# A gated state-space and MLP mix with its gradients on one core: the inverse scratch in 128-partition loads, the first chunk's tables beside the last inverse step, and a new order of loads and buffers in the tail

## The chip, the cores and the metric

The kernel runs on one core of a Trainium2 chip, in one launch. The metric is device time in microseconds, as the median over runs. A profiled execution gives the trace, whose span runs from the first to the last instruction.

## The reference

With `x = A_u` (2048 rows of 448), the reference computes a gate, a state-space long convolution and a squared-ReLU MLP, and the gradients of their mix:

```python
g = sigmoid((x * gate_w).sum(-1, keepdims=True))
# a: K[d, l] = Re sum_n C[d,n] exp(dt A[d,n] l) dt B[d,n],  N = 256, l < 2048
y = irfft(rfft(x, 4096) * rfft(K, 4096))[:2048]        # per channel d, causal convolution
a = bf16(y) + x * Dskip
# b: h = x' @ w1 + b1 (448 -> 1792);  b = relu(h)**2 @ w2 + b2 (1792 -> 448)
out = g * a + (1 - g) * b
```

Returned are `out` and 14 gradients for a given `grad_out`: those of `A_u`, of the real and imaginary parts of A, B and C (448 x 256 each), of `log_dt`, `Dskip`, `w1`, `b1`, `w2`, `b2` and `gate_w`.

## The kernel before

The convolutions go by a Fourier transform in two steps of 64 points as matmuls. `fwd1` multiplies the rows and stores its result to a DRAM scratch `gd`, which `load_s1` reads back in another order; `fwd2` (L253) makes the spectrum. A product with another spectrum follows, then `inv1` (L289), which stores to a scratch `hd`; `load_hs` (L300) reads `hd` back in four parts, and `inv2` (L307, L309) makes the rows of the output from them. The MLP's forward and backward pass is cut into "dense steps" (`N_(n)` does n units of them, `D_` as many as bring it to a quota): L651 and L654 are matmuls, L666 and L679 the evacuations on ScalarE, L687 a second group of matmuls.

Three stages follow one another.

*The front* (to about 215 us) loads inputs and tables and transforms the input and the weighted gradient. A scheduler sets the order of its instructions. The inverse transform of the kernel gradient, `inv1(q)` for q = 0 to 3, has dense steps between its parts. Then `tc.manual_schedule()` starts, and from there each engine does its instructions in the order in which the code names them.

*The middle* makes, in 14 chunks of states, the convolution kernel and the sums over positions for the parameter gradients. For each chunk, `load_x` (L1012) and `load_y` (L1017) read a record of powers, `neg_x` (L1020) and `seeds_x` (L1023) start the table X on ScalarE, `step_x` doubles it on VectorE (L991, L992, L994); `fields_y` (L1028 to L1035) copies fields on ScalarE, `seeds_y` (L1043) and five `build_y` (L1001, L1002, L1004) make the table Y. `kgen` (L1066) multiplies the tables into the convolution kernel, `k_out` (L1077) stores it to `k_d`, and `load_yt` (L1085, "LY") transposes Y with four DMA transposes on SP's queue. `step_sums` (L1166) is the `inv2` of the inverse transform in a form that picks the rows wanted: it reads all four parts of `hd`, evacuates (L1173) and passes the result through `dk_d` to the buffer DK. The opening of the middle does chunk 0 and half of chunk 1 by hand; then `period(c, tokens)` runs a list of tokens: Y0 to Y4, X0 to X2, KM, KO, LY, the sums Z0 to Z3, P0, P1, and D for dense steps.

*The tail* (from about 665 us) reads the finished kernel from `k_d` (`reload_k`, L1310 and L1316), transforms it (`fwd1`, L206 and L207 evacuate, L232 multiplies, L237 stores), runs the last chunk's LY and sums, and then for each q: `product` (L1478, L1479), `fwd2` of the next part, `back1` (an `inv1`). `back1(0, q)` stores the output's half, `back1(1, q)` the gradient's. Its staging buffers are four blocks `oq`. Output loop 0 (L1538, L1539, L1546 to L1551) makes out_0 and the gate's sums from `hs1`, with `ao = oq[q]` as its output buffer; output loop 1 (L1564) makes the gradient of `A_u` from `hs2`, with the parameter gradients (`param_grads`, L1395 to L1429) between as `Pg(n)`, which need `load_raw` (L1373) and `load_st` (L1379) for four blocks of channels. `load_rows16` (L351) fetches the gradient `Gt` and the input `U` again.

Of the kernel before, what the change touches and what calls it, by code (L numbers as in the profile page):

```python
# [19 lines left out]
P = 128  # L20
# [22 lines left out]
def host_consts():  # L43
# [42 lines left out]
    Et = np.zeros((2, 32, 2, 4, 8, 32), np.float64)  # L86
    k1 = np.arange(32)[:, None]
    l1 = np.arange(32)[None, :]
    for hp in range(2):
        for l0g in range(4):  # L90
            for x in range(8):
                l = 64 * l1 + 16 * l0g + 8 * hp + x
                C = (2.0 / 4096) * np.exp(2j * np.pi * (k1 + 0.5) * l / 4096)
                Et[hp, :, 0, l0g, x] = C.real
                Et[hp, :, 1, l0g, x] = -C.imag
    c["Etw"] = Et.reshape(128, 4 * 8 * 32)
# [29 lines left out]
def sum_consts():  # L126

    mats, places = {}, position_places()
    k1 = np.arange(32)
    for l, v in enumerate(rounded_positions()):  # L130
        l0 = l % 64
        C = (2.0 / 4096) * np.exp(2j * np.pi * (k1 + 0.5) * l / 4096)
        p, b = places[int(v)]
        e, i = (p // 2 % 2, 2 * (p // 4) + p % 2) if p < 16 else (p // 8, p % 8)
        row = 8 * sum_row(b) + i
        M = mats.setdefault((l0 % 8, l0 // 16, e, row // 32), np.zeros((2, 32, 2, 32)))
        M[l0 // 8 % 2, :, 0, row % 32] += C.real
        M[l0 // 8 % 2, :, 1, row % 32] -= C.imag
    keys = sorted(mats)
    return np.concatenate([mats[k].reshape(128, 32) for k in keys], axis=1), keys  # L140
# [22 lines left out]
class Ker:  # L163
# [133 lines left out]
    def load_hs(self, hd, q, hs):  # L297
        for hp in range(2):
            src = bass.AP(tensor=hd, offset=(32 * hp + 8 * q) * D, ap=[[64 * D, 64], [1, 8 * D]])
            self.nc.sync.dma_start(hs[64 * hp:64 * hp + 64].rearrange("p g x d -> p (g x d)"), src)  # L300

    def inv2(self, hs, q, x, hp, ps, more=()):

        nc = self.nc
        Et = self.Et[:].rearrange("p (g x m) -> p g x m", g=4, x=8)
# [9 lines left out]
def kernel(ctx, tc, A_u, A_A_re, A_A_im, A_B_re, A_B_im, A_C_re, A_C_im, A_log_dt, A_Dskip,  # L315
# [30 lines left out]
    def load_rows16(queues, dst, ap2d, halves=(0, 1)):  # L346

        for g in range(NG):
            for h in halves:
                src = bass.AP(tensor=ap2d.tensor, offset=ap2d.offset + (16 * g + 8 * h) * D, ap=[[64 * D, 32], [1, 8 * D]])  # L350
                queues[g % len(queues)].dma_start(flat(dst[32 * g:32 * g + 32, 8 * h:8 * h + 8]), src)  # L351
# [10 lines left out]
    cs["F1K"] = cs["F1BD"].reshape(4, 32, 256).transpose(1, 0, 2).reshape(128, 256)  # L362
# [12 lines left out]
    for h in range(2):  # L375
        for g in range(NG):
            src = bass.AP(tensor=u2.tensor, offset=u2.offset + (16 * g + 8 * h) * D, ap=[[64 * D, 32], [1, 8 * D]])
            (nc.sync if g % 2 == 0 else nc.scalar).dma_start(flat(U[32 * g:32 * g + 32, 8 * h:8 * h + 8]), src)
    ldb = const.tile([P, D], bf16, name="ldb")
# [86 lines left out]
    Fs = K.t("F17", [P, 8704])  # L466
# [80 lines left out]
    Fp = K.t("F17", [P, 8704])  # L547
# [412 lines left out]
    KW = K.t("K28", [P, 2 * NA * D])  # L960
    DK = KW[:, NA * D:].rearrange("p (a d) -> p a d", d=D)
    Y = K.t("Y16", [P, W2, 2, 64])
    XB = K.t("X16", [P, 8192])
    RB = K.t("R32", [P, 8, 2048])
    XW = [XB[:, 0:4096], RB[:, 4:6].rearrange("p k x -> p (k x)")]
    yring = [RB[:, k].rearrange("p (w n) -> p w n", n=P) for k in range(4)]
    KS = XB[:, 4096:4096 + NY * 80].rearrange("p (s c i q) -> p s c i q", s=NY, q=GC, i=CW)
    zrow = XB[0:48, 7680:8128]
    G_.memset(zrow, 0.0)
    nc.sync.dma_start(bass.AP(tensor=k_d, offset=16 * 48 * D, ap=[[D, 48], [1, D]]), zrow)  # L970
    G_.memset(Y[:].rearrange("p w t b -> p (w t b)").bitcast(fp32), 0.0)
    G_.memset(Y[:, :, 0, 0], 1.0)
    Fv = K.t("F17", [P, 8704])
# [21 lines left out]

    yb, vb = Y[:, 0, 0, 0:1], Vt[:, 0:1]

# [9 lines left out]
    Y4 = Y[:]  # L1007
# [3 lines left out]
    def load_x(c):  # L1011
        nc.sync.dma_start(rx_[:, 0:896], bass.AP(tensor=rec_d, offset=c * P * RS, ap=[[RS, P], [1, 896]]))  # L1012

    def load_y(c):
        nonlocal rec
        rec = K.t("rec", [P, 1024])
        nc.sync.dma_start(rec[:], bass.AP(tensor=rec_d, offset=c * P * RS + 896, ap=[[RS, P], [1, 1024]]))  # L1017
# [132 lines left out]
    def load_rows():  # L1150
        load_const("Ew", nc.sync)
        for b in (KW[:, 0:3584], KW[:, 3584:7168], R2[:, 0:3584], R2[:, 4096:7680]):
# [32 lines left out]

    R2 = RB.rearrange("p k x -> p (k x)")
    load_x(0)
    load_y(0)
    load_rows()
    for h in range(2):  # L1190
        G_.memset(KW[64 * h + 32:64 * h + 64, NA * D:].bitcast(fp32), 0.0)
    for i in range(3):
        fields_y(i)
# [24 lines left out]
    for v in range(3):  # L1218
        step_x(1, 2 << v, v)
        N_(1)  # L1220
    load_x(2)
    while acc[1]:
        N_(1)
    BK.update(h=("N0", "N1"), t="N2", a="N3")
    Pt = K.t("P14", [P, 7168])
# [62 lines left out]
    def period(c, tokens, k=0):  # L1288
        for o in tokens:
# [3 lines left out]
            elif c or o not in ("YS", "Y0", "Y1", "Y2", "Y3", "Y4", "LY"):  # L1293
                token(o, c)
    for lb in range(4):
        nc.sync.dma_start(dbt[lb], bass.AP(tensor=DBT_d, offset=lb * P * 2048, ap=[[2048, P], [512, DT], [1, 512]]))
    period(0, "KM KO D D D".split())
    period(1, "SP YS Y0 D Y1 Y2 WP Z0 D NX Y3 Y4 Z1 D KM KO Z2 L0 D Z3 L2 R P0 D SA P1 D X0 FY0 D S X1 D FY1 FY2 D X2 D WD".split())
    Fx, R2 = Fv, RB.rearrange("p k x -> p (k x)")
# [18 lines left out]
    def reload_k():  # L1318
        reload(64, 64, 0, 2, 32, (2, 4), (48, 16))
        reload(32, 32, 0, 4, 8, (4, 2), (48, 16))  # L1320
        reload(64, 64, 3, 1, 48 + 32, (2, 4), (48, 16))
        reload(32, 32, 7, 1, 48 + 8, (4, 2), (48, 16))
        fix(79, 16, 4, 3, 34, 2)
        fix(47, 16, 2, 7, 12, 20)
# [27 lines left out]
    period(NCH - 1, "LY P0 SA P1 S WD".split())  # L1352
# [12 lines left out]
    sx[0, 2] = load_sx(0, 2, 4)  # L1365
    Gt = Yf[:, 0:7168].rearrange("p (t d) -> p t d", d=D)
# [84 lines left out]
    M2v = Yf[:, 0:4096]  # L1451
    K.M2 = M2v

    def between(n):
        if n == 5:
            nc.sync.dma_start(M2v, cdr["M2"].ap())
    K.fwd1(lambda j: xv[:, JO.index(j)], gd[2], stage=stg + [K.t("st", [P, 4, D], bufs=2) for _ in range(2)], between=between)
    period(NCH, "Z0 Z1 Z2 P0 Z3 P1".split())
    sums = back_s(NCH - 1, [Qs.pop((NCH - 1, h)) for h in range(2)])
    s1k = [b.rearrange("p (a d) -> p a d", d=D) for b in (KW[:, 7168:10752], KW[:, 10752:14336], SB[:, 6272:9856], SB[:, 0:3584])]  # L1460
    for q in range(4):
        K.load_s1(gd[2], q, s1k[q])
# [8 lines left out]
    oq = [Fx[:, 1792 * i:1792 * i + 1792].rearrange("p (a d) -> p a d", d=D) for i in range(4)]  # L1471
# [16 lines left out]
    for q in range(4):  # L1488
# [8 lines left out]
        if q == 2:  # L1497
            load_st(0, SB[:, 9856:11904], G_)
            Pg(1)
            load_rows16((nc.sync,), Gt, G2, (0,))  # L1500
    hs1.append(load_hs(1, 0, 6))
    load_rows16((nc.sync,), Gt, G2, (1,))
    for q in range(4):
# [23 lines left out]
    for q in range(4):  # L1527
        hs = hs1[q]
        ao = oq[q]
        for x in range(2):  # L1530
            pp = K.pair()
            for hp in range(2):
# [4 lines left out]
                jk = XB[:, 7168 + 448 * (t % 2):7616 + 448 * (t % 2)]  # L1537
                V.scalar_tensor_tensor(out=jk, in0=ps, scalar=1.0, in1=Gt[:, t, :], op0=ALU.mult, op1=ALU.mult, accum_out=dg[:, t:t + 1])  # L1538
                V.scalar_tensor_tensor(out=ao[:, 2 * hp + x], in0=ps, scalar=g32[:, t:t + 1], in1=b0, op0=ALU.mult, op1=ALU.add)  # L1539
# [75 lines left out]
```

## Time and profile before

| | us |
|---|---|
| median of 3 runs (857.14 to 860.26) | 859.49 |
| profiled execution | 860.13 |
| its span | 858.4 |
| busy: PE, DVE, ACT, POOL | 642.5, 565.5, 514.1, 155.8 |
| DMA traffic | 181.59 MB, mean 212 GB/s |

PE is TensorE's matmuls, PEld its weight loads, DVE is VectorE, ACT ScalarE, POOL GpSimd, and SPq the queue of SyncE, which only issues DMAs here. Names such as L1166 are lines of the kernel before. In a line of waits, "A x <- B y: 13.7, 1, 13.7" says that A's instruction waited for B's: total us, times, the longest. In a timeline the columns are start, duration, engine, line, operation, output<-input and the number of instructions. PEclk is the granted TensorE clock as a share of full speed (0.852 in the mean); a DMA share of 1 means that all 16 DMA engines are busy.

### The profile page before, as it was taken

What the parts mean: (1) busy time and instruction counts of PE and PEld (TensorE: products, weight loads), DVE (VectorE), ACT (ScalarE), POOL (GpSimd) and SP (SyncE); (2) the same over time, 40 slices, a digit from 0 to 9 for tenths busy, and PEclk for the clock granted to TensorE, in tenths of its full rate; (3) what the DMA queues carried; (4) which work ended last, traced back from release to release, by engine and by line L of the source; (5) the groups of instructions that cost most, each with busy time, mean ns of one, the idle gap of its engine ahead of it and who ended that gap; (6) DMA issues with size and microseconds to landing.
All of it is one profiled execution on the core that took longest, in us unless ns stands there. A gap on an engine that the chain in (4) does not pass through costs nothing.

```text
span 858.4 us, 20221 instructions
## 1 busy us (share of the span) xinstructions
PE 642.5 (75%) x8433; PEld 337.7 (39%) x8477; DVE 565.5 (66%) x932; ACT 514.1 (60%) x869; POOL 155.8 (18%) x262
## 2 busy tenths in 40 slices
PE   3577957879467987997999976987999732973483
PEld 1122323323234554564655653544656411531011
DVE  4596686775733287958998985575779233692674
ACT  1596876686345774885788766774555123882153
POOL 3222101112414010111101020100001230115242
PEclk9977965988869998998999995997999965997556
DMA  9957667558979399999889989796997597979992
GB/s 185 244 146 251 230 227 285 199 203 290 241 144 240 69 261 198 251 207 201 195 202 214 182 194 215 142 189 138 189 217 204 133 218 251 390 210 288 257 305 59
DMA packets 209547, 181.59 MB, mean 212 GB/s; under 512 B 132160, under 2 KB 185993, under 8 KB 209199
## 3 DMA queue, kind: packets, MB, share of 16 engines
q1 hardware_dynamic: 187838, 124.93, 62.4%
q0 software_dynamic: 13408, 35.22, 14.2%
q10 hardware_dynamic: 8208, 20.14, 6.7%
q8 instruction: 66, 1.08, 0.5%
q14 instruction: 27, 0.21, 0.1%
HBM read 85.19 MB, written 64.32 MB: 174 GB/s over the span
## 4 chain that ended last, share of the span: by engine, by line
PE 35%; DMA 22%; DVE 14%; ACT 14%; issue 9%; SPq 3%; POOL 1%; ACTq 0%; POOLq 0%; DVEq 0%
PE psN L880 7%; PE psN L651 5%; PE psS L1138 4%; DMA R<-Y 3%; DMA hd<-F 3%; PE psX L1066 3%; PE psN L687 2%; DMA U<-rT_d 2%; SPq L1085 2%; DMA gd<-X 2%; DVE Y L1001 2%; PE psF L1110 1%; PE psX L687 1%; DVE F L1002 1%; DMA F<-rec_d 1%
## 5 line engine op out<-in xcount | busy, mean ns | idle before, releaser
L1112 ACT CAST P<-psF 128x1024 bf16<-128x1024 f32 x56 | 57.2, 1021 | 11.2 <-PE psF L1110 11.0
L687 PEld LDWEIGHTS <-U 128*128 128x128 bf16 x448 | 41.5, 101 | 40.5 <-issue 10.8
L651 PE MATMUL psN<-S 128*128 128x512 bf16 x151 | 47.3, 418 | 10.6 <-ACT st L1173 3.3
L1001 DVE TENSOR_TENSOR Y<-Y,F 128x1024 bf16<-128x1024 bf16 (+3 forms) x70 | 48.0, 686 | 3.1
L651 PEld LDWEIGHTS <-S 128*128 128x128 bf16 x336 | 30.4, 102 | 49.5 <-issue 25.2
L1004 DVE TENSOR_TENSOR Y<-Y,F 128x1024 bf16<-128x1024 bf16 (+3 forms) x70 | 48.1, 687 | 2.4
L687 PE MATMUL psN<-S,U 128*128 128x449 bf16 x224 | 47.9, 355 | 0.0
L1002 DVE TENSOR_TENSOR F<-Y,F 128x1024 bf16<-128x1024 bf16 (+3 forms) x70 | 47.3, 676 | 0.0
L1110 PE MATMUL psF<-S,R 41*128 41x32 bf16 x1792 | 32.0, 175 | 18.4 <-DVE S L1096 10.6
L1145 POOL DMA_DIRECT2D s_d<-st x28 | 14.0, 506 | 167.4 <-ACT st L1143 161.3
L880 PEld LDWEIGHTS <-U 128*128 128x128 bf16 x308 | 29.1, 102 | 32.1 <-issue 8.0
L880 PE MATMUL psN<-D,U 128*128 128x448 bf16 x168 | 39.8, 388 | 2.4 <-ACT U L865 2.1
L1110 PEld LDWEIGHTS <-R 41*128 41x128 bf16 x1792 | 27.7, 94 | 30.3 <-issue 26.4
L679 ACT ACTIVATE U<-psN 128x1024 bf16<-128x1024 bf16 x37 | 38.1, 1031 | 1.3 <-PE psN L678 1.3
L1043 DVE COPY Y<-rec 128x256 bf16<-128x256 bf16 x14 | 10.3, 737 | 42.3 <-PE psX L1066 24.1
L666 ACT ACTIVATE U<-psN,b_f 128x512 bf16<-128x512 f32 x44 | 28.6, 685 | 14.7 <-DVE st L535 7.5
L687 PE MATMUL psX<-D,U 128*128 128x448 bf16 x144 | 36.0, 391 | 0.7 <-ACT D L693 0.7
L1121 DVE TENSOR_TENSOR M<-P,X 128x2048 bf16<-128x2048 bf16 x14 | 17.1, 1221 | 26.9 <-ACT P L1112 26.9
L232 PEld LDWEIGHTS <-cb_F1BD 128*128 128x128 bf16 x96 | 10.3, 117 | 55.2 <-issue 45.4
L651 PE MATMUL psN<-K,S 128*128 128x512 bf16 x99 | 27.9, 394 | 4.8 <-issue 3.5
L865 ACT ACTIVATE U<-U 128x1792 bf16<-128x1792 bf16 x12 | 20.1, 1694 | 15.7 <-DMA U<-rT_d 15.7
L880 PE MATMUL psN<-S,U 128*128 128x448 bf16 x140 | 28.4, 353 | 0.0
(356 smaller groups left out, 1690.1 us busy)
## 6 DMA issues: line engine op xcount, KB each, us to landing
sp<-K ACTq DMA_DIRECT2D x8, 896.0 KB, 5.8
R<-hd SPq DMA_DIRECT2D x12, 448.0 KB, 13.7
U<-rT_d SPq DMA_DIRECT2D x6, 896.0 KB, 6.6
rT_d<-U POOLq DMA_DIRECT2D x10, 512.0 KB, 4.8
hd<-F SPq DMA_DIRECT2D x11, 448.0 KB, 12.8
U<-rT_d SPq DMA_DIRECT2D x9, 512.0 KB, 6.4
X<-gd SPq DMA_DIRECT2D x5, 896.0 KB, 4.8
U<-dhT_d SPq DMA_DIRECT2D x5, 896.0 KB, 5.7
```

Of the source, the lines that this page charges most:

```text
L651: T_.matmul(pss[k][:], lhsT=w[:, dt], rhs=x(2 * half + k)[:, dt], start=(dt == 0), stop=False, skip_group_check=True)
L666: S.activation(r[:, 512 * lb:512 * lb + 512], pss[k][:], ACT.Relu, bias=b1_f[:, j:j + 1])
L679: S.activation(hn[j % 2][:, 8 * th:8 * th + 8, :], ps[:], f)
L687: T_.matmul(ps[:, 0:w], lhsT=hn[j % 2][:, t, :], rhs=rhs[:, t, :], start=(t == 0), stop=(t == LT - 1))
L880: T_.matmul(ps[:, 0:D], lhsT=src[:, j, P * x:P * x + P], rhs=ws[:, j, :], start=(w == 1 and j == 0), stop=(j == FT - 1))
L1001: V.tensor_tensor(out=run(yb, dst, [64, X2], [d0[1], n // d0[1]], [1, d0[1]]), in0=run(yb, 0, [64, X2], *src), in1=pr, op=ALU.mult)
L1002: V.tensor_tensor(out=run(vb, 0, [n, X2], [d0[1], n // d0[1]], [1, d0[1]]), in0=run(yb, 0, [64, X2], *src), in1=pi, op=ALU.mult)
L1004: return V.tensor_tensor(out=hi, in0=hi, in1=run(vb, n, [2 * n, W2], [-n, 2], [1, n]), op=ALU.add)
L1066: T_.matmul(ps[32 * g:32 * g + 32, i], lhsT=run(xb, 2048 * (1 - t) + w, [W2, 32]), rhs=Y[:, w, t, 0:NY], start=(h == 0 and t == 0), stop=( ...
L1110: T_.matmul(psz[:, t, 32 * b:32 * b + 32], lhsT=yt[64 * t:64 * t + NY, b, :], rhs=DKc[64 * t:64 * t + NY, c % 2, 16 * (j % 2) + b].rearran ...
L1112: S.copy(run(zbs[c, h][:, 0:1], 16 * (j % 2), [1024, 2], [64, NA], [32, 2], [1, 16]), run(psz[:, 0, 0:1], 0, [512, 2], [1, NA], [NA, 2], [ ...
L1138: T_.matmul(sps[64 * h:64 * h + 64, cc, r, :], lhsT=Q[h][r][:, 1024 * t + 64 * a:1024 * t + 64 * a + 64], rhs=(nident if r == 0 and t == 1 ...
```

## The change

1. `load_hs` reads a part of `hd` in one DMA over 128 partitions, where there were two over 64. The table `Et` is padded with zeros to 128 rows for each half (2048 columns for 1024), and `inv2`'s matmuls read 128 rows instead of 64. `step_sums` gets its table in the same row order.
2. The input's rows are divided between the two queues as halves instead of alternately, and two buffers change their size or home.
3. The last inverse step is moved behind the start of the manual order; `load_x(0)`, `load_y(0)`, `neg_x` and two of the three table steps of chunk 0 are placed in it. The scratch parts 2 and 3 go to another buffer. The clearing of Y is split between VectorE and POOL. `load_x(1)` and `load_y(1)` go to POOL's queue. All five `build_y` with a dense step each, and the rest of the dense steps of the opening, come before `neg_x`, `seeds_x(1)` and `step_sums`; `kgen(0)` and `k_out` follow the sums directly. `period(0)` has only dense steps.
4. In the tail, the reloads have their two outer dimensions exchanged, with the table of the first transform permuted accordingly. The LY of the last chunk moves from before the transform to after it. The table M2 and one part of `gd` are loaded on POOL's queue. `Gt` and `oq` exchange buffers. Three parts of `hs1` are read before the second half of Gt, and three of `hs2` before output loop 0. `load_raw` and `load_st` of blocks 1 to 3 move from the `back1(1, q)` loop into output loop 0. The rows of Gt and U are divided between SP and POOL. In output loop 0, each VectorE operation of L1539 becomes a ScalarE copy with a scale, and one VectorE addition follows for each pair of tiles.

```diff
     def load_hs(self, hd, q, hs):
-        for hp in range(2):
-            src = bass.AP(tensor=hd, offset=(32 * hp + 8 * q) * D, ap=[[64 * D, 64], [1, 8 * D]])
-            self.nc.sync.dma_start(hs[64 * hp:64 * hp + 64].rearrange("p g x d -> p (g x d)"), src)
+        src = bass.AP(tensor=hd, offset=8 * q * D, ap=[[32 * D, P], [1, 8 * D]])
+        self.nc.sync.dma_start(hs.rearrange("p g x d -> p (g x d)"), src)
...
-            nc.tensor.matmul(ps[32 * l0g:32 * l0g + 32], lhsT=Et[64 * hp:64 * hp + 64, l0g, 2 * q + x, :],
-                             rhs=hs[64 * hp:64 * hp + 64, l0g, x, :],
-                             start=not more, stop=True, tile_position=(64 * hp, 32 * l0g), skip_group_check=bool(more))
+            nc.tensor.matmul(ps[32 * l0g:32 * l0g + 32], lhsT=Et[:, hp, l0g, 2 * q + x, :], rhs=hs[:, l0g, x, :],
+                             start=not more, stop=True, tile_position=(0, 32 * l0g), skip_group_check=bool(more))
...
-    for q in range(4):
-        if q < 3:
-            spectra(q + 1)
+    for q in range(3):
+        spectra(q + 1)
...
+    load_x(0)
+    load_y(0)
     neg_x()
-    for v in range(3):
-        tables_x(0, v)
+    def early(q2):
+        N_(IV[q2])
+        if q2 == 0:
+            tables_x(0, 0)
+            tables_x(0, 1)
+    K.inv1(Pc, 3, hd[0], between=early)
...
+    load_rows()
+    V.memset(Y[:, :, 0, 0], 1.0)
+    V.memset(Y[:, :, 1, 0], 0.0)
+    G_.memset(Y[:, :, :, NY:64], 0.0)
+    for i in range(3):
+        fields_y(i)
...
+    tables_x(0, 2)
+    load_x(1, G_)
+    N_(1)
+    seeds_y()
+    load_y(1, G_)
+    for v in range(5):
+        build_y(v)
         N_(1)
-    load_x(1)
-    seeds_y()
-    load_y(1)
+    while acc[1]:
+        N_(1)
     neg_x()
     seeds_x(1)
-    for v in range(2):
-        build_y(v)
-        N_(1)
     step_sums()
-    for v in range(2, 5):
-        build_y(v)
-        N_(1)
+    kps0 = kgen(0)
+    k_out(0, kps0)
     YTs[0] = [load_yt(j) for j in range(4)]
...
-    period(0, "KM KO D D D".split())
+    period(0, ["D"] * nd)
...
-        reload(64, 64, 0, 2, 32, (2, 4), (48, 16))
-        reload(32, 32, 0, 4, 8, (4, 2), (48, 16))
+        reload(64, 64, 0, 2, 32, (48, 16), (2, 4))
+        reload(32, 32, 0, 4, 8, (48, 16), (4, 2))
...
-    period(NCH - 1, "LY P0 SA P1 S WD".split())
+    period(NCH - 1, "P0 SA P1 S WD".split())
...
-    Gt = Yf[:, 0:7168].rearrange("p (t d) -> p t d", d=D)
+    Gt = Fx[:, 0:7168].rearrange("p (t d) -> p t d", d=D)
...
+    period(NCH - 1, ["LY"])
+    G_.dma_start(M2v, cdr["M2"].ap())
...
+    for q in range(4):
+        K.load_s1(gd[2], q, s1k[q], G_ if q == 0 else None)
     period(NCH, "Z0 Z1 Z2 P0 Z3 P1".split())
...
-    oq = [Fx[:, 1792 * i:1792 * i + 1792].rearrange("p (a d) -> p a d", d=D) for i in range(4)]
+    oq = [Yf[:, 1792 * i:1792 * i + 1792].rearrange("p (a d) -> p a d", d=D) for i in range(4)]
...
         back1(1, q)
-        if q < 3:
-            hs1.append(load_hs(1, q + 1, (4, 0, 1)[q]))
-        if q == 2:
-            load_raw(2, SB[:, 6272:7808], G_)
-            load_st(2, SB[:, 7808:9856], G_)
-    load_raw(1, SB[:, 3584:5120], G_)
-    load_st(1, SB[:, 9856:11904], G_)
-    load_raw(3, SB[:, 0:1536], G_)
-    load_st(3, SB[:, 1536:3584], G_)
+        if q == 0:
+            hs1.append(load_hs(1, 3, 1))
+    for q in range(3):
+        hs2.append(load_hs(2, q, (2, 5, 3)[q]))
...
-                V.scalar_tensor_tensor(out=ao[:, 2 * hp + x], in0=ps, scalar=g32[:, t:t + 1], in1=b0, op0=ALU.mult, op1=ALU.add)
-        hs2.append(load_hs(2, q, (2, 5, 3, 6)[q]))
-        if q == 3:
-            load_rows16((nc.sync,), Uv, u2)
+                S.activation(ao[:, 2 * hp + x], ps, ACT.Copy, scale=g32[:, t:t + 1])
+            V.tensor_tensor(out=ao[:, x:x + 3:2], in0=ao[:, x:x + 3:2], in1=br[0][:, 2 * q + x:2 * q + x + 9:8], op=ALU.add)
+        if q == 0:
+            hs2.append(load_hs(2, 3, 6))
+        if q < 3:
+            rw, sb = ((3584, 9856), (6272, 7808), (0, 1536))[q]
+            load_raw(q + 1, SB[:, rw:rw + 1536], G_)
+            load_st(q + 1, SB[:, sb:sb + 2048], G_)
+        if q == 2:
+            load_rows16((nc.sync, G_), Uv, u2)
```

More of the change, by code (lines that the diff above doesn't have):

```diff
@@ L361 @@
     cs["Ew"], ekeys = sum_consts()
-    cs["F1K"] = cs["F1BD"].reshape(4, 32, 256).transpose(1, 0, 2).reshape(128, 256)
+    krow = np.array([p if p < 32 else p // 32 * 32 + (p % 16) * 2 + p // 16 % 2 if p < 64 else 64 + (p % 16) * 4 + p // 16 % 4 for p in range(P)])
+    cs["F1K"] = np.zeros_like(cs["F1BD"])
+    cs["F1K"][krow] = cs["F1BD"].reshape(4, 32, 256).transpose(1, 0, 2).reshape(128, 256)
     ct, cdr = {}, {}
@@ L959 @@
     order.enter_context(tc.manual_schedule())
-    KW = K.t("K28", [P, 2 * NA * D])
-    DK = KW[:, NA * D:].rearrange("p (a d) -> p a d", d=D)
-    Y = K.t("Y16", [P, W2, 2, 64])
+    K.cmul(Pc, spw[:, 3], spw[:, 2], True, RA[:, 10752:10752 + 2 * 2 * D], parts=2)
     XB = K.t("X16", [P, 8192])
-    RB = K.t("R32", [P, 8, 2048])
-    XW = [XB[:, 0:4096], RB[:, 4:6].rearrange("p k x -> p (k x)")]
-    yring = [RB[:, k].rearrange("p (w n) -> p w n", n=P) for k in range(4)]
+    Fv = K.t("F17", [P, 8256])
+    XW = [XB[:, 0:4096]]
     KS = XB[:, 4096:4096 + NY * 80].rearrange("p (s c i q) -> p s c i q", s=NY, q=GC, i=CW)
[L968 to L973, printed above, removed]
     Vt = Fv[:, 0:2048]
@@ L1184, in step_sums @@
             qe.dma_start(DK[64 * cpy + 40:64 * cpy + 41, 0], bass.AP(tensor=dk_d, offset=640 * D, ap=[[D, 1], [1, D]]))
[L1186 to L1193, printed above, removed]
     def tables_x(c, v):
@@ L1219 @@
         step_x(1, 2 << v, v)
-        N_(1)
     load_x(2)
[L1222 to L1225, printed above, removed]
+    zrow = XB[0:48, 7680:8128]
+    G_.memset(zrow, 0.0)
+    nc.sync.dma_start(bass.AP(tensor=k_d, offset=16 * 48 * D, ap=[[D, 48], [1, D]]), zrow)
     P2 = K.t("M8", [P, 4096])
@@ L1449 @@
     stg = [XB[:, o:o + 1792].rearrange("p (a d) -> p a d", d=D) for o in (0, 1792, 4096, 5888)]
-    M2v = Yf[:, 0:4096]
+    M2v = Fx[:, 0:4096]
     K.M2 = M2v
[L1454 to L1457, printed above, removed]
+    K.fwd1(lambda j: xv[:, JO.index(j)], gd[2], stage=stg + [K.t("st", [P, 4, D], bufs=2) for _ in range(2)])
+    period(NCH - 1, ["LY"])
+    G_.dma_start(M2v, cdr["M2"].ap())
+    s1k = [b.rearrange("p (a d) -> p a d", d=D) for b in (KW[:, 7168:10752], KW[:, 10752:14336], SB[:, 6272:9856], SB[:, 0:3584])]
+    for q in range(4):
+        K.load_s1(gd[2], q, s1k[q], G_ if q == 0 else None)
+    sx[0, 2] = load_sx(0, 2, 4)
     period(NCH, "Z0 Z1 Z2 P0 Z3 P1".split())
     sums = back_s(NCH - 1, [Qs.pop((NCH - 1, h)) for h in range(2)])
-    s1k = [b.rearrange("p (a d) -> p a d", d=D) for b in (KW[:, 7168:10752], KW[:, 10752:14336], SB[:, 6272:9856], SB[:, 0:3584])]
-    for q in range(4):
-        K.load_s1(gd[2], q, s1k[q])
     for w, q, k in ((0, 3, 0), (1, 0, 1), (1, 1, 2)):
@@ L1506 @@
         back1(1, q)
[L1507 to L1515 removed]
+        if q == 0:
+            hs1.append(load_hs(1, 3, 1))
+    for q in range(3):
+        hs2.append(load_hs(2, q, (2, 5, 3)[q]))
     K.st_more = []
```

72 lines of the change are left out of this document (41 added, 31 removed).

## The prediction, made before the changed kernel ran

> **What bounds the kernel now.** I read the slices first. TensorE is busy 75% of the span, but not evenly: it dips around 230 us and through the last eighth, and there its clock is low and DMA is full.
>
> ```profile
> PE   3577957879467987997999976987999732973483
> PEclk9977965988869998998999995997999965997556
> DMA  9957667558979399999889989796997597979992
> ```
>
> Each digit is 21.5 us. The windows view then gives the stages (its columns: length, busy time of PE, its weight loads, DVE, ACT, POOL, then PE clock, DMA share, GB/s):
>
> ```profile
> 225.00:239.20 14.20, 0.54 (x9) 0.19 (x2) 13.65 (x22) 2.05 (x5) 0.00 (x0) 0.64 0.84 199
> 672.40:685.50 13.10, 7.09 (x38) 3.46 (x36) 4.61 (x11) 1.60 (x3) 3.98 (x7) 0.90 0.50 79
> 695.00:709.90 14.90, 0.08 (x2) 0.04 (x1) 0.60 (x2) 0.62 (x2) 0.62 (x1) 0.56 1.11 261
> 726.70:763.50 36.80, 31.55 (x356) 17.44 (x356) 27.43 (x19) 32.18 (x62) 4.42 (x8) 0.94 0.95 341
> 763.50:781.60 18.10, 13.09 (x107) 5.90 (x106) 14.14 (x19) 10.99 (x21) 8.73 (x16) 0.91 0.90 230
> 781.60:799.20 17.60, 0.07 (x4) 0.10 (x1) 0.00 (x0) 0.00 (x0) 4.52 (x8) 0.61 1.05 306
> 799.20:822.40 23.20, 14.53 (x73) 3.03 (x72) 19.52 (x58) 3.83 (x12) 6.53 (x13) 0.50 0.90 255
> ```
>
> Three stretches have an idle TensorE: 225–239, 695–710 and 782–799 us. The waits view names what ended each:
>
> ```profile
> ACT F L1020 <- DMA F<-rec_d: 14.3, 1, 14.3
> PE psN L1166 <- ACT U L666: 13.7, 1, 13.7
> ...
> ACT X L206 <- DMA gd<-X: 15.7, 1, 15.7
> PE psN L232 <- ACT X L206: 14.8, 1, 14.8
> ...
> DVE F L1539 <- DMA hd<-F: 18.0, 1, 18.0
> ```
>
> First: ScalarE's `neg_x` (L1020) stands behind chunk 1's table load, and the dense step's L666 behind `neg_x`. Second: the forward transform has no free staging buffer, because its stores sit on SP behind four DMA transposes. Third: the output loop's buffer F is still being stored. SP's timeline shows the second cause:
>
> ```profile
> 681.85 17.07 SPq L1085 DMA_TRANSPOSE R<-Y  x4
> 699.02 2.46 SPq L1340 DMA_DIRECT2D U<-sp  x1
> 701.59 2.81 SPq L237 DMA_DIRECT2D gd<-X  x4
> ```
>
> **Whole-row scratch loads and head: 0 (−1 to +1.5).** Each `load_hs` becomes one DMA for two; its issues (L300) had a median of 0.5 to 0.6 us, none on the chain of waits. The inverse step keeps its count of matmuls, on 128 rows for 64; L1166 has this form already (128 rows, 0.35 to 0.38 us overlapping at full clock), so I take no change. The padded table adds 256 KB, about 1.3 us at the 212 GB/s mean if nothing hides it. The regrouped input queues carry the same bytes.
>
> **Middle: −10 (−3 to −15).** Chunk 0's tables move beside inverse step 3, chunk 1's loads go to POOL's queue, and `neg_x` and `seeds_x(1)` come after all five `build_y`, each with a dense step. The 13.7 us stall has no cause left there. Seven or so dense steps now precede the sums instead of five: two at about 1.9 us of PE, 3.8 us, fill the hole; they aren't lost from later quotas, as `period(0)` only has to reach the same total. The rest is DVE's: `build_y` costs 10.5 us and the tables of chunk 0 a little over 7, and the latter now run under PE's inverse step. Given back: `neg_x`, the seeds, `k_out` and `fields_y` (0.4 + 0.6 + 3.6 us and the evacuation) stand on ScalarE ahead of the next dense step: 3.5 us. So 13.7 − 3.5 ≈ 10. The lower end is a stall that mostly returns on another wait; the upper is all of 13.7 plus some of the 3.5 us gap at 249–252.
>
> **Forward transform of the gradient: −11 (0 to −14).** The reload of `k_d` has its dimensions swapped, outer 16 instead of outer 2 or 4; the first took 5.86 us (chain, `F<-k_d`) while the DMA share was 0.50: −2.5. [...] The transposes go behind the stores, so the 14.9 us stall goes. But they become serial: without the stall PE's last matmul work (3.31 us in the 12.1 us stage after it, evacuations 6) ends near 695 + 7 − 2.5 = 699.5. SP then issues transposes; 14 such sets took 10.7 to 19.8 us, so with 15 and 2 for landing the last is there at 716.5, and Z3 and the second transform (before at 726.7) wait for it. By the low end this starts at 712, by the high end at 721; a wait of PE for stores as well makes it 726. POOL now carries the M2 table and the first `gd` load, at 0.5 to 0.8 us per issue.
>
> **Products and the gap behind them: −10 (−4 to −13).** From 726.7 to 799.2 DMA's share times length is 0.95·36.8 + 0.90·18.1 + 1.05·17.6 = 69.7 us of 72.5: this stage is DMA-bound. Moved out of it: `load_raw` and `load_st` of blocks 1 to 3 (2.7 MB in rows of 512 B to 1 KB). POOL's queue took 15.8% of 65 us, 10.3, of which by packets I give these 8.5. Then 61 us at a share near 1 is 62: −10. `oq` and Gt swap homes, which changes no bytes, and the loop's buffer F still waits for the last store of `hd` in `oq`, with less traffic ahead of that store; three of the last block's scratch rows are fetched before the output loop instead of in it, 3 times 0.9 MB that by 300 GB/s would be 9 us, but these lie behind the stores on SP's queue and I count them beside the loop. If DMA's share falls to 0.93 instead, −4 to −7.
>
> [...] After the stall the rows show 0.50 (799–822) against 0.94 before. [...]
>
> **Output loop 0: −6 (−3 to −7.5).** VectorE did 16 times L1538 (0.61) and L1539 (0.68), 20.6 us for a stage of 23.2. L1539 becomes a ScalarE copy with scale (0.53 a tile, L206's row; 8.5 beside its 3.83) and one add of 128x896 per pair (0.62 in L267's kind). VectorE: 19.52 − 10.9 + 8·0.62 = 13.6; ScalarE 12.3; PE 14.53 at half clock. The longest is PE's 14.5; with 2.5 us of handing over, 17.
>
> **Output loop 1 and parameter gradients: +3 (0 to +6).** The 8.5 us of small packets land here. Shares before, 0.90·23.2 + 0.73·26 = 39.9, become 48 of 49 − 6 = 43 us, against which the 3 scratch loads above leave the loop if they land before it (up to 9 us): between nothing and 5 us of excess, so +3. U's rows and Gt's are split over SP and POOL: 14.65 us of issue on SP halve, but they end no wait in the chain.
>
> **A queue against the change.** Six kinds of loads move to POOL, or half of them do (`load_x(1)`, `load_y(1)`, M2, one of `gd`, Gt, U). [...]
>
> **Sum.** 0 − 10 − 11 − 10 − 6 + 3 = −34 on the profiled 860.13 us (span 858.4 and 1.7 around it). That run is 0.6 above the median of 859.49: 826 as a time, rounded.
>
> **Rivals.**
> *Transposes bind* (12%). Z3 waits for a set as slow as 19.8 us plus the stores: the −11 becomes 0. 837. For it: L1085 holds 7.7% of the tail's chain. Against: the median set is shorter.
> *DMA merely moves* (14%). Loops 0 and 1 were at shares of 0.90 and 0.73; if they saturate, the −10 is handed back there: +6 more and −6 lost of the loop: 838.
> *A stall comes back in the middle* (12%). `hs` loads (13.7 us to land) arrive after the dense steps have run out: −10 becomes −2: 834.
> *The whole main loop falls out of phase* (10%), the slower case. Its 13 later periods inherit the dense work and queue order that the new beginning leaves. At 366–392 a period lost 6.4 of 26 us of PE while its transposes held SP; the mean, 47.6 us idle in 300–662 over 14, is 3.4. If the new beginning puts every period in that state, 13·3.0 = 39 and the total is 865. It cancels the gain from 34/13 = 2.6 us a period. Against: the order written for the periods is unchanged, and 420–450 shows PE at 28.5 of 30.
> *The new order does nothing* (4%): stalls come back on other waits, DMA is as full, the wait on F remains, and only the reload's 2.5 us is won: 857.
>
> ```profile
> 366.00:392.00 26.00, 19.62 (x337) 12.52 (x336) 17.85 (x26) 17.74 (x33) 2.86 (x5) 0.95 0.87 219
> 420.00:450.00 30.00, 28.52 (x613) 18.74 (x612) 27.66 (x38) 23.07 (x41) 3.42 (x6) 1.00 0.91 197
> ```
>
> **How the numbers follow.** My forecast holds 48%, its range by the sum's terms 811 to 840, of which the far ends are unlikely together. The first three rivals lie at 834 to 838. The bounds give 806 when every term is at its end and loop 0 gets a better clock; the top of 850 takes in two rivals at once (837 + 8 and more). Outside lie the phase rival, the last, and what exceeds every bound. A measurement of this kernel can tell about 0.5%, 4.3 us: faster means under 855, and that is all cases but the phase rival and part of the last: 0.86; the last is half within 0.5% with a little of the phase rival: 0.04; slower: 0.10.
>
> **What would show it.** ScalarE's 14.3 us wait on `F<-rec_d` gone, and no wait over 5 us of PE at the sums; stores of `gd` ahead of transposes on SP, PE without a gap over 4 us before Z3, the second transform starting at 712 to 721; the gap before output loop 0 under 10 us; VectorE under 15 us in loop 0. Wrong would be PE idle time in the main loop above 60 us, a POOL issue above 1 us, or the transposes' set above 20 us.

## The result, and the profile after

The changed kernel takes 833.29 us (median of 4 runs, 828.05 to 835.76) against 859.88 for the kernel before beside it: a ratio of 0.9686 (95% interval 0.9633 to 0.9739), 27 us less. The forecast was 826, with a range of 806 to 850. The profiled execution took 828.05 us (span 826.3) and is the quickest of the four, so the stage lengths below add up to 32 us and not to 27.

The slices of the page after, 20.7 us each (PE, its clock, DMA):

```profile
PE   3668957879879977869999975998999823974580
PEclk9988966899989989899999996899999975997685
DMA  9967667557897999799797979878998499999972
```

The hole around 230 us is a single slice of 7 tenths now; the one in the last quarter is still there, as a 2 and a 3. Stages of the kernel after, by the windows view (length, busy PE, its weight loads, DVE, ACT, POOL, PE clock, DMA share, GB/s):

```profile
211.00:223.00 12.00, 11.59 (x88) 5.58 (x89) 11.55 (x17) 10.50 (x18) 11.88 (x9) 1.00 0.97 352
223.00:240.00 17.00, 12.67 (x258) 7.82 (x251) 6.82 (x9) 6.66 (x14) 3.96 (x8) 0.84 1.25 186
...
668.70:684.30 15.60, 0.03 (x2) 0.03 (x4) 0.62 (x1) 1.34 (x2) 2.34 (x4) 0.59 1.07 258
...
749.60:761.60 12.00, 3.70 (x35) 1.59 (x32) 1.80 (x7) 3.51 (x8) 3.75 (x7) 0.80 1.05 378
761.60:787.40 25.80, 12.33 (x65) 2.62 (x64) 12.84 (x42) 12.60 (x27) 11.65 (x22) 0.63 0.82 258
```

The opening of the middle (211 to 240) has no idle stretch over 4.3 us left. The tail still has one of 15.6 us, where it had one of 14.9. The waits view names it (first line, 640 to 705 us), and what goes on at output loop 0 (the others, whole span):

```profile
PE psF L1099 <- DMA R<-Y: 24.5, 3, 15.6
...
PE psF L306 <- ACT Y L1538: 21.8, 3, 11.4
DVE Y L1539 <- ACT Y L1538: 15.6, 8, 9.4
...
ACT Y L1538 <- DVE X L1537: 10.5, 7, 1.9
...
ACT Y L1538 <- DMA hd<-Y: 8.5, 1, 8.5
```

The 11.4 and the 9.4 us begin at 753 us, ahead of the loop's first write at 761.6, and come from the last line, ScalarE's wait for a store of `hd` from its output buffer. So TensorE's gap at the start of the loop, which the prediction wanted under 10 us, is 11.4. L1099 is the first matmul on the last chunk's transposed Y (L1110 before). It waits for the four transposes that now stand behind the stores on SP:

```profile
668.74 3.62 SPq L237 DMA_DIRECT2D gd<-X  x2
672.41 21.41 SPq L1074 DMA_TRANSPOSE R<-Y  x4
694.25 0.36 SPq L243 DMA_DIRECT2D K<-gd  x1
```

With the start of each stage read off the same instructions in both profiles, the difference is:

| stage | before, us | after, us | difference | forecast |
|---|---|---|---|---|
| start to the first store of `hd` | 134.7 | 129.4 | −5.3 | 0 |
| from there to the end of the sums | 111.9 | 99.2 | −12.7 | −10, with the next row |
| from there to the reload | 425.8 | 421.1 | −4.7 | |
| reload to the second transform | 54.2 | 46.9 | −7.4 | −11 |
| second transform to the first write of output loop 0 | 72.5 | 65.0 | −7.5 | −10 |
| output loop 0 | 21.5 | 25.8 | +4.3 | −6 |
| output loop 1 to the end | 37.7 | 38.9 | +1.2 | +3 |
| span | 858.4 | 826.3 | −32.1 | −34 |

The sum is near the forecast, but its terms are not: 22.7 us came before the reload, where 10 had been forecast, and 9.4 in the tail, where 24 had been. This is one profile each; in the five other kernels below with the same front and middle, the reload began 14.6 to 24.1 us earlier than before. The experiments ask which edits did it. Their times are compared with the kernel before as it ran beside them, by the ratio, since that kernel's median was 860 to 866 us in different groups.

### The profile page after: what moved, and what is told of

Same layout as the page of the kernel before. It is cut to its first block, busy times and chain, and to the rows that moved or that the text cites. A ratio compares the mean times of both kernels' runs of the same rounds, so it can differ in the third digit from the quotient of the medians.

```text
span 826.3 us, 20273 instructions
## 1 busy us (share of the span) xinstructions
PE 632.6 (77%) x8477; PEld 335.2 (41%) x8477; DVE 560.4 (68%) x926; ACT 521.9 (63%) x885; POOL 159.8 (19%) x272
## 5 line engine op out<-in xcount | busy, mean ns | idle before, releaser
L1099 PE MATMUL psF<-S,R 41*128 41x32 bf16 x1792 | 32.2, 175 | 35.4 <-DMA R<-Y 25.9
L687 PE MATMUL psN<-S,U 128*128 128x449 bf16 x224 | 50.7, 370 | 5.5 <-issue 5.5
L1099 PEld LDWEIGHTS <-R 41*128 41x128 bf16 x1792 | 27.4, 94 | 47.7 <-DMA R<-Y 28.2
L679 ACT ACTIVATE U<-psN 128x1024 bf16<-128x1024 bf16 x39 | 40.2, 1030 | 0.7 <-PE psN L678 0.7
L880 PE MATMUL psN<-D,U 128*128 128x448 bf16 x168 | 37.9, 375 | 2.8 <-ACT U L865 2.8
L651 PE MATMUL psN<-K,S 128*128 128x512 bf16 x126 | 34.6, 405 | 0.7 <-ACT R L772 0.7
L1110 DVE TENSOR_TENSOR M<-P,R 128x2048 bf16<-128x2048 bf16 x14 | 17.1, 1219 | 25.4 <-ACT P L1101 25.4
L687 PE MATMUL psX<-D,U 128*128 128x448 bf16 x128 | 29.5, 366 | 4.2 <-ACT D L693 4.2
L1127 PE MATMUL psS<-ident,P 128*64 128x128 bf16 x896 | 27.9, 219 | 4.4 <-issue 4.4
L981 DVE TENSOR_TENSOR R<-R,F 128x1024 bf16<-128x1024 bf16 (+1 forms) x14 | 13.4, 959 | 21.9 <-ACT R L1012 21.5
## 6 DMA issues: line engine op xcount, KB each, us to landing
R<-sp SPq DMA_DIRECT2D x5, 896.0 KB, 11.4
```

Of the source, the lines that this page charges most:

```text
L651: T_.matmul(pss[k][:], lhsT=w[:, dt], rhs=x(2 * half + k)[:, dt], start=(dt == 0), stop=False, skip_group_check=True)
L679: S.activation(hn[j % 2][:, 8 * th:8 * th + 8, :], ps[:], f)
L687: T_.matmul(ps[:, 0:w], lhsT=hn[j % 2][:, t, :], rhs=rhs[:, t, :], start=(t == 0), stop=(t == LT - 1))
L880: T_.matmul(ps[:, 0:D], lhsT=src[:, j, P * x:P * x + P], rhs=ws[:, j, :], start=(w == 1 and j == 0), stop=(j == FT - 1))
L1099: T_.matmul(psz[:, t, 32 * b:32 * b + 32], lhsT=yt[64 * t:64 * t + NY, b, :], rhs=DKc[64 * t:64 * t + NY, c % 2, 16 * (j % 2) + b].rearran ...
L1110: V.tensor_tensor(out=run(pr[:, 0:1], 0, [32, 64], [1, 32]), in0=run(zb[:, 0:1], 0, [32, 64], [1, 32]), in1=run(xb, 32 * h, [W2, 64], [1, ...
```

## Experiments: the two halves, and two parts of the front and middle

**The new front and middle with the old tail.** Everything from the second half of the period loop on is that of the kernel before; the scratch loads keep 128 partitions.

```diff
-    Fx = Fv
-    ... (tail of the kernel after)
+    Fx, R2 = Fv, RB.rearrange("p k x -> p (k x)")
+    ... (tail of the kernel before)
```

> The kernel after, with the whole tail of the kernel before (its order of loads, its homes, its reloads, the old output loop); the 128-partition loads stay. In the two profiles the reload of the kernel began 22.7 us earlier after the change, and the tail from there on took 9.4 us less. If the two parts add up, this kernel takes 859.5 - 22.7 = about 837 us, and its tail from the first reload to the end takes the 186 us of before. Rival, that the tail's new order is what makes the whole: over 850.

Measured: 832.51 us (829.82 to 837.8), ratio 0.9644 (0.9597 to 0.9692). That is the whole gain of the change, without its tail.

**The old kernel with the new tail**, by the opposite edit.

> The kernel before, with the tail of the kernel after. By the same sum 859.5 - 9.4 = about 850 us, of it 7 us won between the first reload and the second transform, 7.5 in the products and 4 lost in output loop 0. Rival, that the tail's gain depends on what the middle leaves behind: within 3 us of before.

Measured: 862.79 us (860.2 to 869.41), ratio 0.9997 (0.9965 to 1.0029): nothing, to 3 us. In its profile the tail took 184.2 us, against 186.0 before: 5.6 less up to the second transform, 1.5 less in the products, 4.3 more in output loop 0, 1.2 more behind it. So the tail's own edits nearly cancel. The tail of the kernel after takes 176.6 us, and that of the first experiment, all in the old order, 178.2; what the tails of those two have in common and this one lacks is the 128-partition load.

**ScalarE's order alone.** In the kernel before:

```diff
     load_y(1)
-    neg_x()
-    seeds_x(1)
     ...
     for v in range(2, 5):
         build_y(v)
         N_(1)
+    neg_x()
+    seeds_x(1)
```

> The kernel before, where only neg_x and seeds_x(1) move on ScalarE from ahead of the first build_y of the opening to behind the last one; the sums come after five dense steps as before. Theory: the 13.7 us stall is a matter of ScalarE's order alone, so it goes, and the kernel ends 9 to 13 us earlier, 847 to 851 us. Rival: the sums then wait for something else of the same length (the scratch loads, VectorE's tables), and the gain is under 4 us.

Measured: 853.89 us (846.08 to 858.81), ratio 0.9856 (0.9801 to 0.9911): 12 us less, with an uncertainty of 5. By the times, two lines moved behind the dense steps are the largest part of the change that was tried alone. The profile doesn't show where the 12 us come from. It is of the slowest of the six runs, 858.81 us; in it the 13.7 us wait is gone, and TensorE waits for the scratch loads instead:

```profile
PE psN L1166 <- DMA R<-hd: 4.8, 2, 4.0
PE psN L1166 <- DMA K<-hd: 1.9, 1, 1.9
```

The sums end at 240.7 us there, 5.9 earlier than before, and the reload begins only 0.9 earlier. So in that run about half of the stall came back as the rival said, on loads of 64 partitions. (The two lines stand behind the sums here, and ahead of them in the change.)

**The input's queues alone.** In the kernel before:

```diff
-            (nc.sync if g % 2 == 0 else nc.scalar).dma_start(flat(U...), src)
+            (nc.sync if g < 2 else nc.scalar).dma_start(flat(U...), src)
...
-                queues[g % len(queues)].dma_start(...)
+                queues[g * len(queues) // NG].dma_start(...)
```

> The kernel before, where only the rows of the input and of the gradient are divided between the two queues as halves and not alternately. In the two profiles the first store of hd came 5.3 us earlier after the change, and ScalarE's wait for the table MI was 0.5 us and not 5.4. Theory: the queues' division does this, so the kernel ends 4 to 6 us earlier, about 854.5 us. Rival: it is a chance of the transfers that differs from run to run, or the other buffers of the front: within 1.5 us of before.

Measured: 858.82 us (853.31 to 862.95), ratio 0.9966 (0.993 to 1.0003): 3 us, at the edge of what can be told. The profiles bear it out. The first store of `hd` came at 132.4 to 134.7 us in the three kernels with the alternating division, and at 126.9 to 130.0 in all those with halves. ScalarE's wait for the table MI tells where, first before, then in this kernel:

```profile
40.00 0.42 ACT L415 ACTIVATE nMI<-cb_MI 128x256 bf16<-128x256 bf16 x1 [5.39 <-DMA cb_MI<-c_MI]
33.82 0.42 ACT L415 ACTIVATE nMI<-cb_MI 128x256 bf16<-128x256 bf16 x1 [0.23 <-DMA cb_MI<-c_MI]
```

The number in brackets is the idle time before the instruction. ScalarE stood there 5.39 us before and 0.23 in this kernel. The load of this small table stands on SP behind the input's rows and six transposes; it was issued at 30.7 us before, at 27.4 in this kernel and at 28.0 after. The bytes ahead of it are the same, but they went faster. In the windows 8 to 14 and 14 to 20 us the DMA share is 1.01 to 1.06 in every kernel; the three with the alternating division moved 196 to 220 GB/s there, all with halves 233 to 258. With halves the two queues begin with partitions 0 to 31 and 64 to 95; alternating, with 0 to 31 and 32 to 63. Whether this makes the rate wasn't tested.

## Experiments: the partitions of the scratch loads, and the moved small loads

**Two DMAs of 64 partitions again**, in the kernel after, into the same places:

```diff
-        src = bass.AP(tensor=hd, offset=8 * q * D, ap=[[32 * D, P], [1, 8 * D]])
-        self.nc.sync.dma_start(hs.rearrange("p g x d -> p (g x d)"), src)
+        for hp in range(2):
+            src = bass.AP(tensor=hd, offset=(8 * q + 2048 * hp) * D, ap=[[32 * D, 64], [1, 8 * D]])
+            self.nc.sync.dma_start(hs[64 * hp:64 * hp + 64].rearrange("p g x d -> p (g x d)"), src)
```

> The kernel after, with each scratch load as two DMAs over 64 partitions again (rows 0 to 63 and 64 to 127), into the same places. From the second transform to the first write of output loop 0 the profiles show 72.5 us before, 71.0 with the tail's change alone (64 partitions), 66.8 with the head's and the middle's alone (128 partitions) and 65.0 after. New theory: the 128-partition form of the loads wins some 5 us there, not the moved small loads, so this kernel's stage takes 70 to 71 us and the time is 4 to 7 us over after, 837 to 840. The prediction's theory, that the form costs and brings nothing: 64 to 66 us, and no difference in time.

Measured: 839.62 us (835.92 to 842.74), ratio 0.9737 (0.9691 to 0.9782), against 0.9686 after. The intervals of these two ratios overlap, so the times alone don't show the 4 to 6 us. The stages do. The one from the second transform to output loop 0 took 69.8 us, against 65.0; it took 69.8 to 72.5 in all five kernels with 64 partitions and 60.8 to 66.8 in all nine with 128. The sums took 11.7 us, against 6.2 to 6.3 in all nine, and ended at 234.8 us, against 228.6 after. The windows view shows why. First the kernel after, then this one, while the four parts of `hd` are loaded for the sums:

```profile
212.00:216.00 4.00, 3.59 (x24) 1.82 (x24) 3.69 (x9) 4.00 (x9) 3.94 (x4) 1.00 1.02 327
216.00:220.00 4.00, 4.00 (x26) 1.83 (x24) 3.93 (x5) 2.93 (x5) 3.94 (x2) 1.00 1.02 383
220.00:224.00 4.00, 4.00 (x55) 2.27 (x58) 2.93 (x5) 2.65 (x4) 4.00 (x5) 1.00 1.01 398
```

```profile
212.00:216.00 4.00, 4.00 (x26) 1.96 (x25) 3.69 (x8) 4.00 (x9) 3.94 (x4) 0.98 1.01 242
216.00:220.00 4.00, 4.00 (x27) 1.99 (x26) 3.90 (x6) 2.54 (x4) 3.95 (x2) 1.00 1.06 223
220.00:224.00 4.00, 4.00 (x42) 1.97 (x44) 2.51 (x4) 2.65 (x4) 3.84 (x5) 1.00 1.01 219
```

Read the last two columns together. The DMA engines are fully busy in both (shares of 1.01 to 1.06), but move 327 to 398 GB/s with loads to 128 partitions and 219 to 242 with loads to 64 (all traffic of the window). With 64 partitions the rate is 0.62 of the other in the mean; by these rows the same bytes hold the engines 1.6 times as long. Why the rate differs isn't shown.

**The small loads back in the products stage.** In the kernel after:

```diff
         if q == 0:
             hs1.append(load_hs(1, 3, 1))
+        if q == 2:
+            load_raw(2, ...); load_st(2, ...)
+    load_raw(1, ...); load_st(1, ...)
+    load_raw(3, ...); load_st(3, ...)
...
-        if q < 3:
-            load_raw(q + 1, ...); load_st(q + 1, ...)
```

> The kernel after, with load_raw and load_st of blocks 1 to 3 issued again where the kernel before does, in and behind the back1(1, q) loop. The prediction's theory: the stage from the second transform to output loop 0 is bound by DMA, and these loads hold 8.5 us of it, so it goes from 65 us to 72 to 74 while the output loops lose at most 3: 838 to 842 us. New theory, by the profiles named for the scratch loads: they are worth under 2 us there, and the output loops get as much back, since POOL's queue no longer mixes them with out_0's stores: within 3 us of after.

Measured: 835.13 us (830.3 to 839.51), ratio 0.9686 (0.9639 to 0.9732), the same as after. The stage took 66.4 us, 1.4 more; the four kernels with these loads moved and the transposes where the change has them took 64.1 to 65.2. The 8.5 us that the prediction took out of this stage by moving those loads are not there. One reason is that not all of them left it: in the kernel after, POOL gets to block 1's loads before the others are in the loop, and issues them at 749.4 to 753.4 us, ahead of the loop's first write at 761.6. Only blocks 2 and 3, 1.4 of the 2.3 MB, came into the loop.

## Experiments: output loop 0

**The sum on VectorE again**, in the kernel after:

```diff
-                S.activation(ao[:, 2 * hp + x], ps, ACT.Copy, scale=g32[:, t:t + 1])
-            V.tensor_tensor(out=ao[:, x:x + 3:2], in0=ao[:, x:x + 3:2], in1=br[0]..., op=ALU.add)
+                V.scalar_tensor_tensor(out=ao[:, 2 * hp + x], in0=ps, scalar=g32[:, t:t + 1], in1=b0, op0=ALU.mult, op1=ALU.add)
```

> The kernel after, with output loop 0's scaled sum on VectorE again (one operation per tile, no ScalarE copy and no pair addition). The loop took 21.5 us before and 25.8 after, where ScalarE's copy starts 0.05 us after VectorE's read of the same tile ends, and VectorE's addition waits for that copy. Theory: the split makes the two engines take turns, so the old form brings the loop back to 21 to 22 us and the kernel gains about 4, 829. The prediction's theory, that VectorE's 20.6 us bind the old form and the split wins time: the loop gets longer than 25.8 us or stays.

Measured: 827.28 us (824.23 to 834.28), ratio 0.9607 (0.9558 to 0.9656). The loop took 21.3 us. The split costs 4.3 to 4.5 us: the loop took 25.8 in every profile that has it with the addition in place, and 21.3 to 21.5 in every one without it.

**The pair's addition one pair later**, in the kernel after:

```diff
-            V.tensor_tensor(out=ao[:, x:x + 3:2], in0=ao[:, x:x + 3:2], in1=br[0]..., op=ALU.add)
+            add_late((q, x))    # the addition of the pair before; for x = 1 its stores too
...
+    add_late()                  # the last one, ahead of output loop 1
```

> The kernel after, with the same operations in output loop 0, but each pair's addition (and behind it out_0's store) is issued after the reads of the next pair's tiles, so VectorE doesn't stand waiting for ScalarE's copy. Theory of taking turns: a pair then costs VectorE 3 times 0.55 us, PE at half clock 14.5 us in all binds, and the loop takes 16 to 19 us instead of 25.8: 7 to 9 us less, 825. Rival, that the loop waits for its DMA or for PE at half clock: over 23 us.

Measured: 822.32 us (816.1 to 827.54), ratio 0.953 (0.9479 to 0.9582), with the loop at 18.7 us. Together with the last experiment, which can't be told from it, this is the best version found: another 1.6% over the change. ScalarE's and VectorE's timelines of the kernel after show the turns that it takes apart:

```profile
763.33 0.62 DVE L1537 SCALAR_TENSOR_TENSOR X<-psF,F 128x448 bf16<-128x448 f32 x1
763.99 0.64 ACT L1538 ACTIVATE Y<-psF,g 128x448 bf16<-128x448 f32 x1 [1.24 <-DVE X L1537]
765.82 0.62 DVE L1537 SCALAR_TENSOR_TENSOR X<-psF,F 128x448 bf16<-128x448 f32 x1 [1.87 <-PE psF L308]
766.49 0.63 ACT L1538 ACTIVATE Y<-psF,g 128x448 bf16<-128x448 f32 x1 [1.87 <-DVE X L1537]
767.16 0.63 DVE L1539 TENSOR_TENSOR Y<-Y,K 128x896 bf16<-128x896 bf16 x1 [0.70 <-ACT Y L1538]
```

ScalarE only reads the tile in psF after VectorE has read it (763.33 + 0.62, then 763.99); VectorE, whose next reads stand behind the addition, then waits 0.70 us for ScalarE's result. In these rows each ScalarE read starts 0.04 to 0.05 us after the end of the VectorE read, and the profile puts ScalarE's idle time before it, 1.24 and 1.87 us, down to that read; whether the two could read at once isn't shown. No engine was over 12.9 us busy in the loop's 25.8. With the addition later, only the first of the two turns is left, and TensorE's two waits inside the loop for psF fall from 5.5 and 4.9 us to 3.0 and 1.7.

## Experiments: the transposes, and the early tables

**The transposes ahead of the stores**, in the kernel after:

```diff
-    period(NCH - 1, "P0 SA P1 S WD".split())
+    period(NCH - 1, "LY P0 SA P1 S WD".split())
...
-    period(NCH - 1, ["LY"])
```

> The kernel after, with the last chunk's four transposes ahead of the forward transform's stores on SP's queue again. After, TensorE waits 15.6 + 4.3 + 4.5 us for them behind the transform; before, it waited 14.8 for a staging buffer and 9.8 for the second transform's rows. From the first forward matmul to the second transform the profiles show 41.2 us before and 37.9 after. Theory: the place of the set moves a wait and hardly shortens it, so the stretch is 39 to 42 us here and the time within 4 us of after. The prediction's theory: the serial order wins 8 us, so this kernel takes some 841.

Measured: 834.23 us (829.87 to 838.31), ratio 0.9651 (0.9603 to 0.9699), not told from after. The stretch from the first forward matmul to the second transform was 43.6 us, 5.7 over after, but the products behind it took 61.7 and not 65.0: of the 5.7 us that the new place wins, 3.3 are given back in the next stage.

**The transposes before the reload**, in the kernel after:

```diff
-    period(NCH - 1, ["KM", "KO"])
+    period(NCH - 1, ["KM", "KO", "LY"])
...
-        (nc.sync if xq % 2 else G_).dma_start(xs...)   # reload and fix
+        G_.dma_start(xs...)
...
-    period(NCH - 1, ["LY"])
```

> The kernel after, with the last chunk's transposes issued on SP as soon as Y is made, before the kernel's reload, and all of the reload on POOL's queue, so that they stand neither before the stores nor behind them. They take 12 to 14 us of SP, as in the chunks before, and are through when the first store comes; the reload takes up to 4 us longer on one queue. Theory, that the set on SP binds the stretch in either order: from the first reload to the second transform it falls from 46.9 us to 32 to 38, and the time to 820 to 826. Rival, that the stretch is bound by DMA as a whole (its share was 0.9 and over): under 3 us of gain.

Measured: 833.42 us (824.02 to 836.09), ratio 0.963 (0.9575 to 0.9684), not told from after, as the rival said; its reason, a stretch bound by DMA as a whole, is not shown, for the share was 0.81 and 0.62 in 659 to 670 and 670 to 682 us. The transposes no longer stand in any wait, and others have come in their place (this kernel's waits from 640 to 705 us, then the second transform's first matmul):

```profile
POOL K L243 <- DMA gd<-X: 12.3, 1, 12.3
...
PE psN L232 <- DMA F<-k_d: 8.4, 2, 7.9
...
705.62 0.96 PE L253 MATMUL psN<-K,F 128*64 128x448 bf16 x4 [17.76 <-DMA K<-gd]
```

The reload, with transposes beside it, comes later, and the second transform waits for loads from `gd`, one of which waited for the stores to land. From the first of the last chunk's stores to `k_d` to the second transform it is 57.6 us, against 54.2 after, and the products give back 4.

**The early tables.** In the kernel after, `tables_x(0, 0)` and `tables_x(0, 1)` are behind the last inverse step:

```diff
         N_(IV[q2])
-        if q2 == 0:
-            tables_x(0, 0)
-            tables_x(0, 1)
...
-    tables_x(0, 2)
+    for v in range(3):
+        tables_x(0, v)
```

> The kernel after, with the first two steps of chunk 0's table X behind the last inverse step again and not between its parts. They are 3.9 us of VectorE. Theory: in the new opening VectorE sets when the dense steps and the sums can go (its busy time was 11.6 of 12 us at 211 to 223), so the sums end up to 4 us later and the kernel takes 2 to 4 us more than after. Rival: dense steps cover it, and there is no difference beyond 1 us in the sums' end (228.6 us).

Measured: 828.02 us (825.9 to 832.07), ratio 0.9584 (0.9534 to 0.9634), with the sums ending at 226.3 us, against 228.6. The early tables win nothing; whether they cost something can't be told, as the two intervals touch.

**Both edits together**, the transposes before the reload and the late addition:

> The kernel after with two edits together: the transposes before the reload, with the reload on POOL, and the pair's addition in output loop 0 behind the next pair's reads. The second alone gave 822.3 us, with the loop at 18.7 instead of 25.8. If the first wins 8 us or more and the two add up, 810 to 815 us; if the stretch is bound by DMA, 820 to 823.

Measured: 824.27 us (816.86 to 826.93), ratio 0.9527 (0.9477 to 0.9576): the late addition's gain and nothing on top.

## Why the prediction was right in its sum and wrong in its terms

*The sum.* 27 us came for 34, and this nearness is in part luck: in the profiles the stages before the reload won 12.7 us more than forecast and the tail 14.6 less. The prediction's bounds for its terms also add up to a wider range than the 811 to 840 it names: 50.5 to 2.5 us less, 810 to 858.

*Whole-row loads and head, 0.* The step that failed by its reasoning. It counted issues and matmuls and bytes, and never asked at what rate a load of 64 partitions moves. The 64-partition form costs 4.8 us of the products stage and 6.2 at the sums' end, of which the kernel's time keeps some 4 to 6 in all, by medians whose intervals overlap. The head's regrouping, put down as "the same bytes", wins about 3: the same bytes moved at 233 to 258 GB/s and not at 196 to 220, and the small table behind them was issued some 3 us earlier.

*Middle, −10.* ScalarE's order did make the stall: with it undone the wait is gone, and 12 us went by the times (0.9856). Whether they went at that place isn't shown, as the one profile has the sums only 5.9 us earlier. Two of the prediction's signs came in the kernel after: ScalarE's wait on `F<-rec_d` fell from 14.3 to 3.3 us, and no wait of TensorE at the sums is over 4.3. The term was undersized for what the new opening brings as a whole. Front and middle gave 0.9644, some 31 us; ScalarE's order, the head and the loads' form make up some 20 of these by their own ratios, if these add up. The early tables are not in the rest. The rest is about 11 us with an uncertainty of 9. The profiles show a place for some of it: from the end of the sums to the reload it is 425.8 to 430.8 us in the four kernels with the old opening, and 418.2 to 424.8 in the eight with the new one that leave the last transposes behind the reload. Which edit does it stays open: the two dense steps more ahead of the sums, `kgen` and `k_out` ahead of the transposes, POOL's queue for chunk 1's loads and the moved buffers weren't tried one by one.

*Forward transform, −11.* The prediction's own working, 726.7 to 716.5, gives 10.2. The stage gave 7.4 in the profile. The reload won 4.1, 9.0 us for 13.1 (forecast 2.5). That the exchanged dimensions bring the 2.5 was the author's estimate, and no run shows it, as none has them alone; in the profiles the loads `F<-k_d` landed after 2.9 us in the median, 3.8 before. The rival of the binding transposes is in part what happened: the set took 21.4 us, beyond the 10.7 to 19.8 that the other sets had shown, and beyond the 20 named as a sign of being wrong, and TensorE stood 15.6 us for it where no gap over 4 was forecast. Why it is slow there is open; DMA's share doesn't tell, being 1.02 to 1.26 during all 14 sets of the kernel after.

*Products, −10.* The number came out as −7.5, but for another cause. The stage was DMA-bound as the prediction said (share 0.99 and 1.05 after); the price of the moved loads was mis-sized, 8.5 us against 1.4. The share of a queue in engine time was taken as time that the stage would lose, the 2.7 MB counted three full blocks where the last is half of one (2.3 MB), and block 1 stayed in the stage. Most of the gain, 4.8 us, was the scratch loads' form, in the same stage and by the same bound.

*Output loop 0, −6.* It became +4.3. The sum of busy times per engine was near (VectorE 12.8 for 13.6 us, ScalarE 12.6 for 12.3, PE 12.3 for 14.5), and "2.5 us of handing over" was not: the loop is a chain through two engines, and for half of its 25.8 us VectorE stands. The 806 at the foot of the range takes in a better clock in this loop. No run shows what would set it: it was 0.50 before, 0.63 after and 0.59 with the late addition, behind waits of TensorE of 20.6, 11.4 and 9.3 us.

*Output loop 1, +3*: +1.2.

*The slower rival* did not come: from the end of the sums to the reload the kernel after took 4.7 us less, not 39 more. POOL's added issues cost nothing that shows: those of chunk 1's loads, M2 and `gd` took 0.54 to 0.56 us. Before, POOL's issues took 0.51 to 0.56 us at 826 to 847 us, with VectorE busy for 19.9 of the 21, and 0.52 at 788 to 790, with it idle.

## What to carry to other kernels

Where DMA's share is near 1, read GB/s beside it: a low rate at a full share (219 to 242 GB/s, against 327 to 398) was here the mark of loads over 64 partitions, and a load over all 128 was worth more than moving small loads out of the stage (4.8 us against 1.4). An instruction that waits for a load belongs behind all work that its engine has ready; two lines moved were worth 1.4%, with an uncertainty of 0.6. Work split between two engines that read the same accumulator tile wasn't done side by side here: put a pair's worth of other work between one engine's result and the other's use of it (this took the loop from 25.8 to 18.7 us).

## What the runs showed of the hardware

At a DMA share of 1.01 to 1.06, in the windows from 212 to 224 us, the transfers went at 219 to 242 GB/s with loads to 64 partitions at a time and at 327 to 398 with loads to 128. The input's rows went at 196 to 220 or at 233 to 258, at the same share (1.01 to 1.06), by how they were divided between two queues. Four DMA transposes of one chunk took 10.6 to 23.3 us of SP's time in the kernel after, at shares of 1.02 to 1.26 that don't sort them. In output loop 0 of the kernel after, ScalarE's read of an accumulator tile never overlapped VectorE's read of the same tile: for the 16 tiles it started 0.04 us or more after that read's end.
